# Attention, then routed experts: the weighted sum of a tile five steps behind its scores, with what goes along

## The chip, the cores and the metric

One core of a Trainium2 chip runs the whole program in one launch. Times are device microseconds of that core. The kernel before has a median of 1753.66 us over three runs (1752.63 to 1756.88).

## The reference

Four batches of 12288 queries (384 x 32 positions, 128 channels) attend to 768 keys each. The keys are the means of 4 x 4 blocks of `kv`, times a 128 x 128 matrix; the values are the same rows.

```
kv_flat = mean of 4x4 blocks of kv, @ w_sr          # [B, 768, 128]
k = v = kv_flat
s = (q @ k.T) / sqrt(128);  a = exp(s - max(s));  a /= sum(a) + 1e-9
x = a @ v                                            # [B * 12288, 128]
do = x @ w_skip > 0;  e = argmax(x @ w_gate);  g = softmax(x @ w_gate)[e]
out = x + do * g * (relu(x @ w1[e]) @ w2[e])         # 8 experts, 1024 hidden
```

The last two lines hold for rows of which `do` is true; the others are `x` itself. Of 49152 rows each goes to one of eight experts or to none.

## The kernel before, in words

A tile is 128 queries, so there are 384 tiles (`NTILE`), 96 in each batch (`TPB`). The work around the change is one loop over steps t (`while t < NTILE + LAG`), whose order on every engine is the order in which the loop writes its instructions. In step t:

- PE computes the scores of tile t (`scores`, six matmuls of 384 columns, since each factor is split in a high and a low half), then the weighted sum of tile t - `LAG` (`attend`, 18 matmuls of 138 columns: 128 value columns, nine projections for routing, one column of ones for the softmax's sum), then transposes the last two of the six key blocks of tile t-1 (`p_transpose`).
- DVE takes the row maximum of tile t (`row_max`), ACT its exponential (`row_exp`).
- Of tile t-1, ACT writes the high halves (f16) of the first four key blocks (`p_hi`), DVE the low halves (`p_lo`); then SP's queue gets a DMA that transposes both into `pt`. `attend` reads `pt` as weights. The pool `ptp` has `LAG` buffers of `pt`; the pool `hl` has four of `p16`, from which the DMA reads.
- The two blocks that PE transposed go to `ptq` for a pair of tiles at once: ACT copies the high halves and DVE subtracts, a step after the second tile of the pair was transposed (`next_a`, `next_v`).
- After each second `attend`, ACT scales the two tiles' sums to rows; after each fourth, SP stores them (`out_dram<-rows`); after each twelfth, a row job (`route`) starts, which ranks the rows of 12 tiles by expert over the following steps, on POOL, DVE and PE, and hands out the scatter of these rows to `scr` (`scatter_next`, one a step, on POOL's queue).
- Queries come in groups of four tiles: `load_q` at each fourth step on SP's queue, `q_split` into high and low halves some steps later.
- The next batch's `kv` comes as 24 loads of 256 KB on SP's queue (`KV_T`: six key blocks of four parts). POOL adds up the blocks (`pool_kv`, from four steps after the last part), and `prep_kv` makes keys and values of them from step 86 of the batch on, one piece a step (`preps`).

Ahead of the loop the first batch's keys are made; its values (`prep_v(0)`: largest key, scale, weight `wv`, two halves of value matmuls) are made in the first steps, one piece a step, and are needed by the first `attend`.

The last steps (t from 384) hold two attends a step and the first matmuls of the expert blocks: 24 peeled blocks of 512 rows of the largest expert (`peel`), then a loop over the rest. `first_step(left)` starts loading and splitting the experts' weights in the last 54 steps.

The lines that matter: `LAG` L66, `prep_v` L597, `p_transpose` L689, `attend` L708, the list of loads L966 and the step loop L977. Matmuls of `scores` are L655 to L657, of `attend` L720; `p_hi` is L673, `p_lo` L677, the transposing DMA L682, PE's transposes L695, the pair's copy and subtraction L702 and L703, the store L738, the value matmuls L591 with their copy L594 and subtraction L526, `wv` L549.

Of the kernel before, what the change touches and what calls it, by code (L numbers as in the profile page):

```python
# [14 lines left out]
AF = mybir.ActivationFunctionType  # L15
ALU = mybir.AluOpType
# [9 lines left out]
def kernel(  # L26
# [11 lines left out]
    nc = tc.nc  # L38
    NR, C, RT, P = q.shape
    B = kv.shape[0]  # L40
# [7 lines left out]
    PEXP = 15  # L48
# [10 lines left out]
    GT = 4  # L59
    GW = GT * P  # L60
    RG = RT // GT
    TPB = NQ // P
    NTILE = B * TPB
    NGRP = NTILE // GT
    XW = C + 10
    LAG = 6  # L66
    WARM = 6
    PREWARM = 7
    PSL = 11
    KD = 4  # L70
    PP = 2
# [352 lines left out]
    with ExitStack() as p1:  # L424
# [172 lines left out]
        def prep_v(b, c0=0):  # L597
            v_max(b, c0, KC)
            yield
            v_weight(b)  # L600
            yield
            yield
            for h in range(2):
                v_matmul(b, h)
                yield

        def prep_kv(b):
            for h in range(2):
                k_matmul(b, h * HC, (h + 1) * HC)
                yield  # L610
            yield from prep_v(b)
# [19 lines left out]
        def q_split(g):  # L631
            q_g = q_sb.pop(g)
            hi = qt.tile([P, GW], F32R, name="q_hi")
            lo = qt.tile([P, GW], F32R, name="q_lo")
            early_a.append(lambda: nc.scalar.copy(hi, q_g))

            def low():
                if g < 3:
                    behind(nc.gpsimd.tensor_tensor(out=lo, in0=q_g, in1=hi.bitcast(F32), op=ALU.subtract))
                    return  # L640
                paced["both"] = nc.vector.tensor_tensor(out=lo, in0=q_g, in1=hi.bitcast(F32), op=ALU.subtract).ins

            early_g.append(low)
            qT[g] = (hi, lo)
# [42 lines left out]
        KP = KC - KD  # L687

        def p_transpose(t):  # L689
            g, j = divmod(t, PP)  # L690
            if j == 0:
                PTP[g] = acc_ps()
            p = p_flat(t)
            for i in range(KP):
                nc.tensor.transpose(PTP[g][:, (j * KP + i) * P:(j * KP + i + 1) * P],  # L695
                                    p[:, (KD + i) * P:(KD + i + 1) * P], ident)
            if j < PP - 1:
                return
            ps = PTP[g][:, 0:PP * KP * P]
            hl_t = ptq.tile([P, 2, PP * KP * P], F16, name="ptq")  # L700
            PTQ[g] = hl_t.rearrange("p a (j k x) -> p a j k x", j=PP, x=P)
            next_a.append(lambda: nc.scalar.activation(out=hl_t[:, 0, :], in_=ps, func=AF.Copy, scale=2.0 ** PEXP))  # L702
            next_v.append(lambda: nc.vector.scalar_tensor_tensor(  # L703
                out=hl_t[:, 1, :], in0=ps, scalar=2.0 ** PEXP, in1=hl_t[:, 0, :], op0=ALU.mult, op1=ALU.subtract))

        AVL = [(k, v, x) for k in range(KC) for v, x in ((0, 0), (0, 1), (1, 0))]

        def attend(t):  # L708
            g, j = divmod(t, GT)
            r, o = divmod(g, RG)  # L710
            v_hi, v_lo, v_sc = *KV[t // TPB][2:4], KV[t // TPB][4][:, 0:1]
            v = (v_hi, v_lo)
            if j % 2 == 0:
                AVT[g] = acc_ps()[:, 0:2 * XW].rearrange("p (a x) -> p a x", x=XW)
            ps = AVT[g]
            pt = PT.pop(t)
            ptq_t = PTQ[t // PP]
            for i, (k, a, x) in enumerate(AVL):
                w = pt[:, x * KD + k, :] if k < KD else ptq_t[:, x, t % PP, k - KD, :]
                nc.tensor.matmul(ps[:, j % 2, :], w, v[a][:, k, :], start=(i == 0), stop=(i == len(AVL) - 1))  # L720
            if j == 0:
                if o == 0:
                    ROWS[r] = rowp.tile([P, RT, XW], F32, name="rows")
            rows = ROWS[r][:, o * GT:(o + 1) * GT, :]
            rs = small.tile([P, 2], F32, name="rs") if j % 2 == 1 else None

            def inverse():
                nc.vector.tensor_scalar(out=rs, in0=ps[:, :, XW - 1], scalar1=1e-9 * 2.0 ** PEXP, scalar2=v_sc,  # L728
                                        op0=ALU.add, op1=ALU.mult)
                nc.vector.reciprocal(rs, rs)  # L730

            def scale():
                for i in (0, 1):
                    c = j - 1 + i
                    nc.scalar.activation(out=rows[:, c, :], in_=ps[:, i, :], func=AF.Copy, scale=rs[:, i:i + 1])
                if j < GT - 1:
                    return
                nc.sync.dma_start(ov[r][:, o * GT:(o + 1) * GT, :], rows[:, :, 0:C])  # L738
                if o == RG - 1:
                    jobs.append([route(r), None])  # L740

            if j % 2 == 1:
                early_v.append(inverse)
                next_l.append(scale)
# [221 lines left out]
        KV_T = {}  # L966
        for nb in range(1, B):
            for i in range(KC * R):
                at = 7 * i // 4 if nb == 1 else (nb - 1) * TPB - 10 + 3 * i
                KV_T.setdefault(at, []).append((nb, *divmod(i, R)))  # L970
        PREP_T = 86
        PAD_T = [t for t in range(LAG, NTILE - 68) if t // TPB == B - 1 or t % TPB >= PREP_T]
        PAD_T = [PAD_T[i * len(PAD_T) // NPAD] for i in range(NPAD)]
        assert len(set(PAD_T)) == NPAD
        alloc["w"] = acc_ps
# [1 line left out]
        t = -1  # L977
        while t < NTILE + LAG:
            t += 1
            b, tb = divmod(t, TPB)  # L980
            live = t < NTILE
            for now, nxt in ((split_a, next_a), (split_v, next_v), (late_a, next_l)):
                now.extend(nxt)
                nxt.clear()
            if live:
                scores(t, range(t == 0, 2))
            for u in (t - LAG,) if live else (2 * t - NTILE - LAG, 2 * t - NTILE - LAG + 1):
                if 0 <= u < NTILE:
                    attend(u)
            if 0 <= t - 1 < NTILE:  # L990
                p_transpose(t - 1)
            if live:
                row_max(t)
            if t == 0:
                next(gate, None)
            run_late(early_a)
            run_late(split_a)
            if 0 <= t - 1 < NTILE:
                p_hi(t - 1)
            run_late(late_a)  # L1000
            if live:
                row_exp(t)
            run_late(split_v)
            run_late(early_v)
            if 0 <= t - 1 < NTILE:
                p_lo(t - 1)
            run_late(early_g)
            if live:
                if t % GT == 0 and t // GT + RG < NGRP:
                    load_q(t // GT + RG)  # L1010
                for nb, k, r in KV_T.get(t, ()):
                    load_kv(nb, k, [r])
                if b + 1 < B and tb == PREP_T:
                    preps.append(prep_kv(b + 1))
                if t in PAD_T:
                    write_pads(*PADS.pop(0))
            first_step(NTILE - t)
            if t == NTILE:
                p_s.close()
                p_kv.close()  # L1020
                first_p.append(p1.enter_context(tc.tile_pool(name="first_p", bufs=HOLD)))
                fill(p1, "fill5", 64)
                alloc_h(p1.enter_context(tc.tile_pool(name="hp1", bufs=1)))
                ps_up = p1.enter_context(tc.tile_pool(name="ps_up", bufs=4, space=PSUM))
                alloc["h"] = alloc["w"] = lambda: ps_up.tile([P, ST], F32, name="up_ps")
            ph = t % GT
            if ph == 1 and t // GT + 2 < NGRP:
                q_split(t // GT + 2)
            taken.clear()
            if live:  # L1030
                scatter_next()
            ranked = run_jobs(ph)
            if not live and (not taken or t >= NTILE + 4):
                scatter_next()
            if preps and not ranked and (ph != 0 or tb < LAG):
                if next(preps[0], "end") == "end":
                    preps.pop(0)
            if live and b + 1 < B:
                for nb, k, r in KV_T.get(t - 4, ()):
                    if r == R - 1:  # L1040
                        pools.append(pool_kv(nb, k))
                if pools and len(taken) < 2 and next(pools[0], "end") == "end":
                    pools.pop(0)
                assert not pools or tb < PREP_T, (t, len(pools))
            if 0 <= t - NTILE < FC // 2:
                next(first)
                next(first)
# [96 lines left out]
```

## Time and profile before

| | us |
|---|---|
| median of three runs | 1753.66 |
| the profiled execution | 1737.34 |
| its span, first to last instruction | 1735.6 |
| DVE busy | 1525.8 (88%) |
| ACT busy | 1265.2 (73%) |
| POOL busy | 1024.7 (59%) |

The span is read in three parts: up to about 23 us the first loads and keys, up to 951 us the steps of the attention loop, then the expert blocks. PE is TensorE's matmuls, PEld its weight loads, SP the queue from which most DMAs are issued. An engine's idle time is the time before an instruction in which it did nothing; the profile names beside it what ended the wait. TensorE's granted clock is 0.999 of full speed over the span.

### The profile page before, as it was taken

Reading aid. Unit: us, or ns where it says so; the run is one execution under the profiler, and the core shown is the slowest. Engines: PE = TensorE matmul, PEld = TensorE weight load, DVE = VectorE, ACT = ScalarE, POOL = GpSimd, SP = SyncE. Lnnn points to the kernel's source line nnn. Section 1 sums busy time; section 2 is a strip of 40 time slices with the busy share of each in tenths; the row PEclk is TensorE's granted clock in tenths of the full one; section 3 lists DMA queues with packets and bytes.
Section 4 is the critical chain, followed back from the end, with each engine's and each line's share of the span. In section 5 each row is a group of like instructions: output and inputs, shape, how many; then the busy total and the mean of one; then the engine's idle time right before and its main releaser. Section 6 shows DMA issues by size and latency. Waiting matters only on the chain.

```text
span 1735.6 us, 51351 instructions
## 1 busy us (share of the span) xinstructions
PE 1703.6 (98%) x18801; PEld 1426.6 (82%) x18801; DVE 1525.8 (88%) x3217; ACT 1265.2 (73%) x2399; POOL 1024.7 (59%) x1292
## 2 busy tenths in 40 slices
PE   6999999999999999999999999999999999999998
PEld 5999999999999989999999777777777777777776
DVE  7989999999999999999999877777888888888887
ACT  4888888888898888888888655555555556666664
POOL 3268878888788888765668445543333333343433
PEclk9999999999999999999999999999999999999999
DMA  8999999999899999999998666222433333333333
GB/s 239 220 242 204 198 199 228 228 200 184 175 194 206 226 218 202 183 199 198 203 202 186 175 193 149 89 83 75 93 102 103 99 97 99 100 107 101 97 99 86
DMA packets 616917, 281.18 MB, mean 162 GB/s; under 512 B 502944, under 2 KB 567072, under 8 KB 616736
## 3 DMA queue, kind: packets, MB, share of 16 engines
q1 hardware_dynamic: 590192, 231.68, 64.5%
q0 software_dynamic: 21504, 38.43, 7.0%
q10 hardware_dynamic: 5040, 8.72, 1.3%
q8 instruction: 106, 1.74, 0.5%
q14 instruction: 75, 0.61, 0.1%
HBM read 85.36 MB, written 79.72 MB: 95 GB/s over the span
## 4 chain that ended last, share of the span: by engine, by line
PE 82%; DVE 11%; DMA 2%; issue 2%; POOL 1%; ACT 1%; SPq 0%; POOLq 0%; DVEq 0%; ACTq 0%
PE acc_ps L311 22%; PE acc_ps L720 17%; PE s_ps L655 6%; PE s_ps L657 6%; PE s_ps L656 5%; PE h_ps L296 5%; PE h_ps L298 5%; PE h_ps L297 5%; DVE nm L663 4%; PE acc_ps L695 4%; PE up_ps L296 2%; PE up_ps L298 2%; PE up_ps L297 2%; DVE p L677 2%; DVE ptq L703 1%
## 5 line engine op out<-in xcount | busy, mean ns | idle before, releaser
L192 POOL DMA_INDIRECT scr<-rows,di x384 | 422.2, 1099 | 170.0 <-DVE nm L663 91.5
L669 ACT ACTIVATE p_sb<-s_ps,nm 128x768 f32<-128x768 f32 x384 | 346.8, 903 | 103.9 <-DVE nm L663 100.9
L192 POOL DMA_INDIRECT out_dram<-o,xin x196 | 201.6, 1029 | 318.5 <-DVE o L323 266.0
L663 DVE TENSOR_REDUCE nm<-s_ps 128x1 f32<-128x768 f32 x384 | 365.2, 951 | 19.0 <-PE s_ps L657 17.4
L299 ACT ACTIVATE h_hi<-h_ps 128x512 f16<-128x512 f32 x384 | 223.9, 598 | 206.9 <-PE h_ps L298 193.3
L720 PEld LDWEIGHTS <-pt 128*128 128x128 f16 x4608 | 274.8, 97 | 64.7 <-issue 63.0
L720 PE MATMUL acc_ps<-v_hi,pt 128*128 128x138 f16 x3072 | 320.1, 224 | 2.7 <-DVE rs L728 1.8
L311 PEld LDWEIGHTS <-h_hi 128*128 128x128 f16 x4608 | 287.6, 98 | 15.6
L655 PE MATMUL s_ps<-k_hi,q_hi 128*128 128x384 f32 x768 | 293.4, 382 | 0.4 <-ACT k_hi L520 0.4
L720 PE MATMUL acc_ps<-v_lo,pt 128*128 128x138 f16 x1536 | 293.0, 223 | 0.0
L677 DVE SCALAR_TENSOR_TENSOR p<-p_sb,p 128x512 f16<-128x512 f32 x384 | 276.9, 721 | 5.6 <-ACT p L673 4.8
L300 DVE SCALAR_TENSOR_TENSOR h_lo<-h_ps,h_hi 128x512 f16<-128x512 f32 x384 | 245.7, 687 | 19.4 <-ACT h_hi L299 17.9
L657 PE MATMUL s_ps<-k_hi,q_lo 128*128 128x384 f32 x768 | 259.4, 338 | 0.0
L656 PE MATMUL s_ps<-k_lo,q_hi 128*128 128x384 f32 x768 | 258.1, 336 | 1.0 <-DVE k_lo L521 1.0
L673 ACT ACTIVATE p<-p_sb 128x512 f16<-128x512 f32 x384 | 242.4, 631 | 12.5 <-DMA pt<-p 9.6
L311 PE MATMUL acc_ps<-w_hi,h_lo 128*128 128x128 f16 x2304 | 222.6, 219 | 0.0
L311 PE MATMUL acc_ps<-w_lo,h_hi 128*128 128x128 f16 x2304 | 210.9, 219 | 0.0
L311 PE MATMUL acc_ps<-w_hi,h_hi 128*128 128x128 f16 x2304 | 210.9, 219 | 0.0
L299 ACT ACTIVATE h_hi<-up_ps 128x512 f16<-128x512 f32 x192 | 114.5, 597 | 109.5 <-PE up_ps L298 100.9
L720 PE MATMUL acc_ps<-v_hi,ptq 128*128 128x138 f16 x1536 | 178.0, 223 | 0.0
L323 DVE SCALAR_TENSOR_TENSOR o<-acc_ps,g_sc,xin 128x128 f32<-128x128 f32 x288 | 81.0, 344 | 104.5 <-PE acc_ps L311 100.8
L720 PE MATMUL acc_ps<-v_lo,ptq 128*128 128x138 f16 x768 | 154.9, 223 | 0.0
(200 smaller groups left out, 3393.7 us busy)
## 6 DMA issues: line engine op xcount, KB each, us to landing
q_sb<-in_q_dram SPq DMA_DIRECT2D x96, 256.0 KB
out_dram<-rows SPq DMA_DIRECT2D x96, 256.0 KB
xin<-scr SPq DMA_DIRECT2D x75, 264.0 KB, 2.9
kvt<-in_kv_dram SPq DMA_DIRECT2D x74, 256.0 KB
w_raw<-in_moe_w_dram SPq DMA_DIRECT2D x26, 512.0 KB, 3.9
scr<-pad ACTq DMA_DIRECT2D x32, 264.0 KB
pt<-p SPq DMA_TRANSPOSE x384
scr<-rows,di POOLq DMA_INDIRECT x384
```

What stands on the lines that cost most here:

```text
L192: ins = nc.gpsimd.indirect_dma_start(out=dst, out_offset=bass.IndirectOffsetOnAxis(ap=ids, axis=0), in_=src, in_offset=None, bounds_check= ...
L299: nc.scalar.activation(out=h["hi"][:, c, :], in_=ps, func=AF.Relu)
L300: paced["by"] = nc.vector.scalar_tensor_tensor(out=h["lo"][:, c, :], in0=ps, scalar=0.0, in1=h["hi"][:, c, :], op0=ALU.max, op1=ALU.subtra ...
L311: m = nc.tensor.matmul(ys[t], h[x][:, k, t * P:(t + 1) * P], w[:, k, :], start=(i == 0), stop=(i == len(terms) - 1))
L655: nc.tensor.matmul(s[:, h, :HK], q_hi, k_hi[:, sl], start=True, stop=False)
L656: nc.tensor.matmul(s[:, h, :HK], q_hi, k_lo[:, sl], start=False, stop=False)
L657: nc.tensor.matmul(s[:, h, :HK], q_lo, k_hi[:, sl], start=False, stop=True)
L663: paced["by"] = nc.vector.tensor_reduce(out=NM[t], in_=S_PS[t][:, :, :HK], axis=AX.XY, op=ALU.max, negate=True).ins
L669: nc.scalar.activation(out=P_SB[t], in_=S_PS.pop(t)[:, :, :HK], func=AF.Exp, bias=NM.pop(t))
L673: nc.scalar.activation(out=P16[t][:, 0, :], in_=p_flat(t)[:, 0:KD * P], func=AF.Copy, scale=2.0 ** PEXP)
L677: paced["both"] = nc.vector.scalar_tensor_tensor(out=p16[:, 1, :], in0=p_flat(t)[:, 0:KD * P], scalar=2.0 ** PEXP, in1=p16[:, 0, :], op0=A ...
L720: nc.tensor.matmul(ps[:, j % 2, :], w, v[a][:, k, :], start=(i == 0), stop=(i == len(AVL) - 1))
```

## The change

- `LAG` is 5. So `attend(t - 5)` stands in step t, the pool of `pt` has five buffers, and the step loop is one step shorter.
- The phases that hang on the attends count from t + 1 instead of t: the split of queries (the first one stays at step 1), the row jobs, the pads, the start-up of the experts, and the steps in which pieces of `preps` may run. The start of a batch's `prep_kv` keeps its step (86); one piece is now allowed in a step that was skipped before.
- Pairs for `ptq` are tiles (1, 2), (3, 4), ... with tile 0 and tile 383 alone, instead of (0, 1), (2, 3), ...
- Loads of the second batch's `kv`: load i comes at step max(7i/4, 5i/2 - 6) instead of 7i/4. The first nine (i = 0 to 8) keep their steps, the last comes at step 51 instead of 40.
- In the first batch the two halves of the value matmuls come a step sooner (one empty piece less).

```diff
-    LAG = 6
+    LAG = 5
...
             v_weight(b)
             yield
-            yield
+            if b > 0:
+                yield
             for h in range(2):
                 v_matmul(b, h)
                 yield
...
         def p_transpose(t):
-            g, j = divmod(t, PP)
-            if j == 0:
+            g, j = divmod(t + 1, PP)
+            if g not in PTP:
                 PTP[g] = acc_ps()
...
-            if j < PP - 1:
+            if j < PP - 1 and t < NTILE - 1:
                 return
-            ps = PTP[g][:, 0:PP * KP * P]
+            sl = slice(0 if g else (PP - 1) * KP * P, (j + 1) * KP * P)
+            ps = PTP[g][:, sl]
...
-            ptq_t = PTQ[t // PP]
+            ptq_t = PTQ[(t + 1) // PP]
...
-                at = 7 * i // 4 if nb == 1 else (nb - 1) * TPB - 10 + 3 * i
+                at = max(7 * i // 4, 5 * i // 2 - 6) if nb == 1 else (nb - 1) * TPB - 10 + 3 * i
                 KV_T.setdefault(at, []).append((nb, *divmod(i, R)))
...
-        PAD_T = [t for t in range(LAG, NTILE - 68) if t // TPB == B - 1 or t % TPB >= PREP_T]
+        PAD_T = [t for t in range(LAG + 1, NTILE - 68) if t // TPB == B - 1 or t % TPB >= PREP_T]
...
-            b, tb = divmod(t, TPB)
             live = t < NTILE
+            t1 = t + 1
+            b, tb = divmod(t1, TPB)
...
-                if b + 1 < B and tb == PREP_T:
-                    preps.append(prep_kv(b + 1))
-                if t in PAD_T:
+                if t % TPB == PREP_T and t // TPB + 1 < B:
+                    preps.append(prep_kv(t // TPB + 1))
+                if t1 in PAD_T:
                     write_pads(*PADS.pop(0))
-            first_step(NTILE - t)
+            if not live:
+                first_step(NTILE - t)
+            elif t1 < NTILE:
+                first_step(NTILE - t1)
...
-            ph = t % GT
-            if ph == 1 and t // GT + 2 < NGRP:
-                q_split(t // GT + 2)
+            ph = t1 % GT
+            if t == 1 or (t > 1 and ph == 1 and t1 // GT + 2 < NGRP):
+                q_split(t1 // GT + 2)
...
-            if preps and not ranked and (ph != 0 or tb < LAG):
+            if preps and (tb == PREP_T + 2 or not ranked and (ph != 0 or t < LAG)):
                 if next(preps[0], "end") == "end":
                     preps.pop(0)
```

## Rows read from the trace of the kernel before

**Rows 1.** The page's first part: busy time, share of the span, instructions

```profile
PE 1703.6 (98%) x18801; PEld 1426.6 (82%) x18801; DVE 1525.8 (88%) x3217; ACT 1265.2 (73%) x2399; POOL 1024.7 (59%) x1292
```

**Rows 2.** Busy time by stretch: length, engines' busy us (instructions), clock, DMA share, GB/s

```profile
0.00:23.00 23.00, 10.33 (x33) 7.26 (x33) 13.19 (x18) 3.32 (x6) 10.99 (x43) 1.00 0.91 334
23.00:40.00 17.00, 14.51 (x112) 12.60 (x112) 15.51 (x28) 14.04 (x25) 5.50 (x6) 1.00 0.61 116
...
60.00:140.00 80.00, 78.90 (x863) 73.11 (x862) 73.31 (x142) 68.42 (x127) 46.25 (x71) 1.00 1.16 239
...
250.00:350.00 100.00, 100.00 (x1098) 93.30 (x1097) 95.45 (x185) 88.67 (x163) 81.33 (x110) 1.00 1.13 227
350.00:450.00 100.00, 99.72 (x1094) 92.80 (x1092) 96.96 (x187) 87.30 (x161) 84.15 (x108) 1.00 0.96 187
...
1600.00:1736.00 136.00, 127.22 (x1443) 92.72 (x1443) 108.34 (x250) 75.84 (x150) 53.37 (x52) 0.98 0.34 95
```

**Rows 3.** Timeline of PE: first matmuls of seven attends, and one transpose

```profile
52.98 0.29 PE L720 MATMUL acc_ps<-v_hi,pt 128*128 128x138 f16 x2
...
119.74 0.29 PE L720 MATMUL acc_ps<-v_hi,pt 128*128 128x138 f16 x2
...
120.83 0.38 PE L695 MATMUL acc_ps<-ident,p_sb 128*128 128x128 f32 x2
...
122.11 0.29 PE L720 MATMUL acc_ps<-v_hi,pt 128*128 128x138 f16 x2
...
125.16 0.29 PE L720 MATMUL acc_ps<-v_hi,pt 128*128 128x138 f16 x2 [0.31 <-DMA pt<-p]
...
308.72 0.29 PE L720 MATMUL acc_ps<-v_hi,pt 128*128 128x138 f16 x2
...
615.67 0.29 PE L720 MATMUL acc_ps<-v_hi,pt 128*128 128x138 f16 x2
...
852.55 0.29 PE L720 MATMUL acc_ps<-v_hi,pt 128*128 128x138 f16 x2
```

**Rows 4.** List of waits, the span: us in total, times, longest us

```profile
ACT p L673 <- DMA pt<-p: 9.6, 16, 1.6
...
PE acc_ps L807 <- POOL oh_all L766: 1.8, 1, 1.8
...
PE acc_ps L720 <- DMA pt<-p: 0.7, 2, 0.4
```

**Rows 5.** Timeline of ACT: five `p_hi` and the idle time before each

```profile
54.37 0.63 ACT L673 ACTIVATE p<-p_sb 128x512 f16<-128x512 f32 x1 [0.92 <-DMA pt<-p]
...
125.19 0.63 ACT L673 ACTIVATE p<-p_sb 128x512 f16<-128x512 f32 x1 [1.40 <-DMA pt<-p]
...
309.86 0.63 ACT L673 ACTIVATE p<-p_sb 128x512 f16<-128x512 f32 x1 [0.65 <-DMA pt<-p]
...
616.14 0.63 ACT L673 ACTIVATE p<-p_sb 128x512 f16<-128x512 f32 x1 [0.22 <-DMA pt<-p]
853.12 0.63 ACT L673 ACTIVATE p<-p_sb 128x512 f16<-128x512 f32 x1 [0.34 <-DMA pt<-p]
```

**Rows 6.** Timeline of the first steps, all engines

```profile
28.55 0.41 ACT L549 ACTIVATE wv<-w_dn,v_x_sc 128x138 f32<-128x138 f32 x1 [0.79 <-DVE v_x_sc L547]
...
30.68 0.58 ACT L702 ACTIVATE ptq<-acc_ps 128x512 f16<-128x512 f32 x1
...
30.83 0.44 PE L695 MATMUL acc_ps<-ident,p_sb 128*128 128x128 f32 x2 [1.53 <-ACT p_sb L669]
...
31.11 0.87 PE L591 MATMUL acc_ps<-wv,pooled 128*128 128x138 f32 x6
...
32.47 0.51 ACT L594 COPY kvf<-acc_ps 128x414 f32<-128x414 f32 x1
...
36.04 0.91 POOL L526 TENSOR_TENSOR v_lo<-kvf,v_hi 128x411 f16<-128x411 f32 x1
```

**Rows 7.** Timeline of PE where attention hands over to the experts

```profile
960.45 0.29 PE L720 MATMUL acc_ps<-v_hi,pt 128*128 128x138 f16 x2 [0.41 <-DMA pt<-p]
```

More of the change, by code (lines that the diff above doesn't have):

```diff
@@ L696, in p_transpose @@
                                     p[:, (KD + i) * P:(KD + i + 1) * P], ident)
-            if j < PP - 1:
+            if j < PP - 1 and t < NTILE - 1:
                 return
-            ps = PTP[g][:, 0:PP * KP * P]
+            sl = slice(0 if g else (PP - 1) * KP * P, (j + 1) * KP * P)
+            ps = PTP[g][:, sl]
             hl_t = ptq.tile([P, 2, PP * KP * P], F16, name="ptq")
             PTQ[g] = hl_t.rearrange("p a (j k x) -> p a j k x", j=PP, x=P)
-            next_a.append(lambda: nc.scalar.activation(out=hl_t[:, 0, :], in_=ps, func=AF.Copy, scale=2.0 ** PEXP))
+            next_a.append(lambda: nc.scalar.activation(out=hl_t[:, 0, sl], in_=ps, func=AF.Copy, scale=2.0 ** PEXP))
             next_v.append(lambda: nc.vector.scalar_tensor_tensor(
-                out=hl_t[:, 1, :], in0=ps, scalar=2.0 ** PEXP, in1=hl_t[:, 0, :], op0=ALU.mult, op1=ALU.subtract))
+                out=hl_t[:, 1, sl], in0=ps, scalar=2.0 ** PEXP, in1=hl_t[:, 0, sl], op0=ALU.mult, op1=ALU.subtract))
         AVL = [(k, v, x) for k in range(KC) for v, x in ((0, 0), (0, 1), (1, 0))]
@@ L716, in attend @@
             pt = PT.pop(t)
-            ptq_t = PTQ[t // PP]
+            ptq_t = PTQ[(t + 1) // PP]
             for i, (k, a, x) in enumerate(AVL):
-                w = pt[:, x * KD + k, :] if k < KD else ptq_t[:, x, t % PP, k - KD, :]
+                w = pt[:, x * KD + k, :] if k < KD else ptq_t[:, x, (t + 1) % PP, k - KD, :]
                 nc.tensor.matmul(ps[:, j % 2, :], w, v[a][:, k, :], start=(i == 0), stop=(i == len(AVL) - 1))
@@ L1043 @@
                     pools.pop(0)
-                assert not pools or tb < PREP_T, (t, len(pools))
+                assert not pools or t % TPB < PREP_T, (t, len(pools))
             if 0 <= t - NTILE < FC // 2:
```

## The prediction

> **What bounds the kernel now.** I began with the page's first part. TensorE (PE) works 98% of the span [rows 1], so a change can only win time by removing the 32 us in which PE does nothing, and it loses time wherever it makes PE wait. The table of busy time by stage says where those 32 us are [rows 2]: 12.7 us before 23 us, 2.5 us between 23 and 40 us, 8.4 us after 1600 us (the span ends at 1735.6 us), and so only 8.4 us in all the rest. The first stage is loading, and the last is the end of the expert loop; the change touches neither. What it can reach is the head from 23 to 40 us, the steps of the attention loop (one tile each, 2.37 us, which is the distance of two attends in [rows 3], 119.74 to 122.11), and the few steps in which that loop hands over to the expert blocks at 951 us.
>
> Then I read the list of waits. The one that bears on the change is not PE's. ACT waits 16 times, 9.6 us in all, 1.6 us at most, for the DMA that transposes the probabilities (`pt<-p`) [rows 4]. `p_hi` of tile u+4 writes over the buffer from which tile u's transpose reads (`hl` has four), so ACT's wait dates the landing of tile u's transpose in the step u+5. Today PE wants that transpose in step u+6, a step later, and hardly ever waits. With LAG 5 it wants it in step u+5, when ACT does.
>
> **The parts of the change.** *Five tiles behind instead of six.* PE issues no instruction less. The place of `attend(u)` is that of `attend(u-1)` today. So the lateness of each transpose is the time of ACT's release [rows 5] minus the start of the attend before it [rows 3]:
> - tile 8: 54.37 - 52.98 = 1.4 us
> - tile 37, the worst: 125.16 (when PE itself waited 0.31 us for it) - 122.11 = 3.1 us
> - tile 113: 309.86 - 308.72 = 1.1 us
> - tile 240: 616.14 - 615.67 = 0.5 us
> - tile 337: 853.12 - 852.55 = 0.6 us
>
> These are the peaks of five bursts; the other eleven waits lie inside the same bursts or are smaller. When PE has been delayed by a burst's peak, everything behind it is delayed alike, so that within one burst the peak counts and not the sum. PE has no slack to make it up. With all five paid the price is 6.7 us.
>
> *Later keys' loads spread.* This edit works against the one before. Loads of the second batch's keys came at steps 0 to 40 and now come at steps 0 to 51; behind the first nine, one every 2.5 steps instead of every 1.75. The first nine keep their steps, so tile 8's burst keeps its cause. Tile 37's burst comes at the end of the dense loads. The share of the DMA engines is 1.16 in 60:140, 1.13 in 250:350, where a load comes every three steps, and 0.96 in 350:450, where the loads run out [rows 2]. The new rate is near that of 250:350, whose worst lateness was the 1.1 us of tile 113. So the first batch pays between 1.4 us (the early burst alone) and 4.5 us (both bursts in full); I take 1.5 us, close to the early burst, since the remaining loads are close to the regime whose peak is smaller than that. The other batches keep their loads: 1.1 + 0.5 + 0.6 = 2.2 us. Together 3.7 us. From this goes what PE loses to the same cause today, 1.1 us in 60:140 [rows 2]. Net +2.6 us, between -1.1 us (no transpose late any more) and 6.7 - 1.1 = +5.6 us with one payment a burst.
>
> *Phases.* The split of q, the pairs of PE transposes, the row jobs, the pads and the start-up of the experts move a step forward together with the attends; the pairs change parity because the attends do. So the buffers in PSUM and the loads of ACT and DVE in even and odd steps keep their distance. One thing doesn't: the store of four finished tiles now comes one step behind the q load on SP's queue, ahead of that step's transpose, where it was two behind. Both stand in front of the transpose of one tile in four. I put no term on it; it is a reason for the upper bound and the slower rival below.
>
> *The head.* Tile 0's pair is now a single, so its copy by ACT and subtraction by DVE move from step 3 (30.68, 0.58 us for the pair [rows 6]) to step 2, at half the width: between 0.29 and 0.58 us, I take 0.4. The first values' matmuls come a step sooner: 0.87 us of PE (31.11) ahead of the scores of tile 3, not tile 4. They need `wv`, which ACT ends at 28.96; the scores of tile 3, queued behind them on PE, would begin at 29.8. PE idles 1.53 us until 30.83 there today, so that delay costs little. But ACT's copy of the values (0.51 us at 32.47) also moves forward, ahead of tile 3's exponential, while the 0.58 us of the pair leave that step. ACT's chain is so later by 0.4 + 0.51 - 0.58 = 0.3 us. PE has one attend more behind it at step 7 than today, 1.09 us (119.74 to 120.83 in [rows 3]), and these few steps are paced by exponentials, not by PE. What idle time is left in which that attend fits I put at 0.4 us; less the 0.3 us it gives -0.1 us. The bounds are -1.1 us (it fits whole) and +0.9 us (the two ACT items delay all that follows). The values themselves are there in time: the last `v_lo` is ready at 36.95 today and would be some 2 us earlier, with the attend at step 5, a step earlier too.
>
> *The hand-over.* After the last scores PE has one attend less to do, 1.09 us, and the end would come sooner by that if nothing else were waited for. But at 960.45 PE has already waited 0.41 us for the transpose of tile 381 [rows 7], and what must happen before it (exponential, split, transpose) follows from the last scores. So the saved attend there mostly turns into waiting: +0.5 us beside the shift counted above, between 0 and +1.1 us. The three steps' jobs that now run at a different place of the expert blocks run beside the 24 peeled expert blocks, all of them ahead of the loop that needs their result, and cost nothing; without that cover they would show as SP waiting ahead of the first block of the loop.
>
> **The sum.** +2.6 - 0.1 + 0.5 = +3.0 us on the profiled execution of 1737.34 us (span 1735.6 us): 1740.3 us. The timed runs have a median of 1753.66 us, 16.3 us or 0.9% above the profiled one; the profile doesn't say where that lies, so I add the same difference: 1756.7 us. What a measurement can tell from no change is 0.3%, 5.3 us; +3.0 us lies inside.
>
> **The rivals.** *The cover holds.* If the spread loads bring every transpose in time, PE loses nothing to them, also not today's 1.1 us, and the attend at the head fits whole: -1.1 - 1.1 = -2.2 us, 1751.5 us. For it: of 384 transposes ACT waited for 16, and the worst came at the end of the dense loads, which are thinned. Against it: tiles 113, 240 and 337 were late under loads that the change doesn't touch. The Trainium skill, page "DMA: Bandwidth & Descriptors", section "Anatomy of one DMA — SWDGE (gpsimd) path", has a rule that would favour this rival: a fixed 2.0 us plus the bytes at 436 GB/s, stated for the GpSimd path. For the 256 KB of one tile it gives an estimate of 2.6 us from issue to landing, little more than a step, in every tile alike; issued at the end of step u+1 and wanted in step u+5, none would be late, and the time would be this rival's, 1751.5 us. The waits on `pt<-p` show some landing three steps later than that, so the trace doesn't agree.
>
> *Every burst charges each of its waits.* On the slower side: PE now stops in the same step as ACT, SP's next transposes are issued later for that, and the next tile is late again instead of being carried by the delay. Then PE pays the 9.6 us of ACT's 16 waits one by one [rows 4], less today's 1.1 us, and the hand-over: 8.5 - 0.1 + 0.5 = +8.9 us, 1762.6 us. For it: the store that now follows the q load closely, and a DMA share above 1.1 through a third of the loop [rows 2]. Against it: while PE waits, the queue drains. It decides from about 6 us of waiting on `pt<-p` by PE upward (5.3 + 1.1 us, less the head and the hand-over), since less is within 0.3%.
>
> *More is saved than the head.* PE's largest single stop in the loop is 1.8 us, for the one-hot rows from GpSimd [rows 4]; it may vanish when the row jobs move, or come back elsewhere (bounds -1.8 and +1.8 us, taken as nothing). For a gain above 5.3 us most of the 8.4 us in the middle would have to go, and nothing in the change aims at them: 1748 us at best.
>
> **How the numbers follow.** The forecast has 0.50, the cover that holds 0.25, the waits charged one by one 0.17, the large gain 0.08. A part of the first reaches over 5.3 us when the second and third peaks are paid in full, and a part of the slower rival stays under it. So: faster 0.09, same 0.69, slower 0.22. Of the range, the lower end is the cover that holds with GpSimd's stop gone as well, 1749.7 us; the upper end is the slower rival and the upper bounds of head and hand-over, +8.9 + 1.0 + 0.6 = 1764.2 us. I say 1749.5 to 1764.5.
>
> **What would show it.** The list of PE's waits should have PE waiting for `pt<-p` some 3 to 5 us in all (0.7 us today [rows 4]), in few pieces, the first near 53 us and one near 310 us, and ACT's 16 waits should go, since PE's stop covers them. Between 60 and 140 us the idle time of PE should not be much above 1.5 us. In the head, attends begin near 34.7 us and scores of tile 7 near 38.6 us. I am wrong if PE waits for `pt<-p` less than 1 us (the cover holds), if it waits over 6 us, or if the time changes at another place, such as GpSimd's one-hot rows or the first block of the expert loop.

## The result, and the profile after

The changed kernel takes 1765.94 us (median of 6 runs, 1763.94 to 1766.99); the kernel before, run beside it on the same chip, takes 1754.25 us (6 runs, 1752.63 to 1756.88). The ratio is 1.0065, with a 95% interval of 1.0052 to 1.0078: slower, by 11.7 us. The prediction said 1756.7 us, 3.0 us over before and no change that can be measured, with a range that ended at 1764.5 us. It was wrong, on the side of the slower rival, whose 1762.6 us is nearer to what was measured.

The profiled execution of after took 1764.59 us (span 1762.9 us). Part 1 of its page (busy time, share, instructions), against [rows 1]:

```profile
PE 1710.9 (97%) x18801; PEld 1428.3 (81%) x18801; DVE 1520.5 (86%) x3218; ACT 1265.8 (72%) x2400; POOL 1017.6 (58%) x1292
```

The table of busy time by stage (stretch, its length, busy time and instructions of PE, PEld, DVE, ACT, POOL, then the granted clock as a share, the DMA share and GB/s), of after, against [rows 2]:

```profile
23.00:40.00 17.00, 14.12 (x106) 12.17 (x107) 14.74 (x29) 13.46 (x24) 6.32 (x6) 1.00 0.60 104
60.00:140.00 80.00, 79.96 (x882) 74.35 (x879) 75.25 (x146) 69.61 (x129) 49.36 (x73) 1.00 1.13 228
140.00:250.00 110.00, 107.32 (x1160) 99.05 (x1159) 99.85 (x200) 92.49 (x172) 83.30 (x115) 1.00 1.03 200
250.00:350.00 100.00, 98.16 (x1067) 91.16 (x1065) 93.55 (x182) 86.40 (x159) 79.25 (x107) 1.00 1.09 216
350.00:450.00 100.00, 99.44 (x1096) 92.53 (x1095) 95.81 (x183) 87.37 (x161) 83.61 (x108) 1.00 0.97 190
450.00:600.00 150.00, 148.10 (x1597) 136.69 (x1596) 139.65 (x275) 128.59 (x237) 116.50 (x158) 1.00 0.97 197
```

In 60 to 140 us PE now idles 0.04 us, less than the 1.1 us of [rows 2]. From there on it idles where it hardly did: 2.7, 1.8, 0.6 and 1.9 us in the next four stretches. The list of waits of after (us in total, times, longest) says for what, against [rows 4]:

```profile
PEld L722 <- DMA pt<-p: 15.8, 23, 3.5
...
PE acc_ps L311 <- issue: 10.5, 15, 1.2
...
PE acc_ps L722 <- DMA pt<-p: 8.4, 10, 3.3
```

PE waits for the transposed probabilities in two places of its pipeline: where it loads them as weights (PEld, 15.8 us) and, when the matmuls before have run out too, in the matmuls (8.4 us). The first figure is the better clock of lateness, the second is nearer to what PE loses. The second line of the fence, 10.5 us in the expert blocks, looked like a part of the loss; the first experiment is about it.

Which transposes were late? I numbered the attends by their weight loads (384 of them) and sorted the 23 waits by the tile: 20 are of tiles whose number is divisible by four, with 15.0 of the 15.8 us. So SP's instructions around such a tile are the place to look. SP's queue of after (start, time, operation, count):

```profile
151.12 1.23 SPq L683 DMA_TRANSPOSE pt<-p  x1
152.40 0.57 SPq L622 DMA_DIRECT2D q_sb<-in_q_dram  x1
153.07 0.39 SPq L740 DMA_DIRECT2D out_dram<-rows  x1
153.56 8.49 SPq L683 DMA_TRANSPOSE pt<-p  x4
```

and the same place in the queue of before:

```profile
141.88 1.37 SPq L621 DMA_DIRECT2D q_sb<-in_q_dram  x1
143.78 1.24 SPq L682 DMA_TRANSPOSE pt<-p  x1
145.11 0.53 SPq L738 DMA_DIRECT2D out_dram<-rows  x1
145.75 5.88 SPq L682 DMA_TRANSPOSE pt<-p  x3
```

In before, a transpose goes out between the load of q and the store of four finished tiles, and the one behind the store is that of tile 49: there the store stands ahead of the tiles that leave a remainder of one when divided by four. In after the two stand one behind the other, and the transpose behind both, the first of the four from 153.56 us on, is that of tile 52. PE's weight loads of after, of tiles 51 and 52 and then of tiles 100, 104 and 116 (in brackets the idle time ahead and its releaser):

```profile
157.70 0.71 PEld L722 LDWEIGHTS <-pt 128*128 128x128 f16 x12 [0.16 <-issue]
160.81 0.71 PEld L722 LDWEIGHTS <-pt 128*128 128x128 f16 x12 [0.90 <-DMA pt<-p]
...
281.38 0.71 PEld L722 LDWEIGHTS <-pt 128*128 128x128 f16 x12 [0.60 <-DMA pt<-p]
291.89 0.71 PEld L722 LDWEIGHTS <-pt 128*128 128x128 f16 x12 [1.04 <-DMA pt<-p]
321.46 0.71 PEld L722 LDWEIGHTS <-pt 128*128 128x128 f16 x12 [1.15 <-DMA pt<-p]
```

A gap of 0.16 us stands there at a tile that waits for nothing, too; eight of the 23 waits are hardly longer than that (0.16 to 0.24 us), and the other fifteen carry the sum. Tile 52's transpose let PE go on at 160.81 us, 7.25 us after SP began to issue it. The DMA packets in the same trace show what stood ahead of it: on SP's queue tile 51's transpose ends at 156.29 us, the q load (128 packets of 2 KB) runs to 157.17 us, the store (512 packets of 512 B) to 157.92 us, and only then come tile 52's packets of 256 B, to about 159.0 us. The two transfers take 1.6 us there, more than the 0.90 us for which PE waits. The Trainium skill, page "DMA: Bandwidth & Descriptors", section "Queues, rings and completion order", states that each DMA engine takes the descriptors of a ring in order. The trace agrees: these packets run in the order in which SP issued them. SP also began the issue 1.2 us after the low halves of tile 52 were ready (152.36 us), since it was issuing the other two until then; no run separates the two delays.

Standing behind a store isn't enough to be late: 94 transposes do, and 13 of them made PE's weight loads wait for more than 0.25 us. The packets give a part of the reason. Between 40 and 975 us there are 58 stops of 1.1 to 2.8 us, in which several packets of SP's queue took over 1 us each, where the median of a transpose's packets is 18 ns. Such a stop falls between issue and use for 46 of the 94, and for 10 of the 13. What causes these stops was not tried.

### The profile page after: what moved, and what is told of

It reads as the page before. It is cut to its first block, busy times and chain, and to the rows that moved or that the text cites. A ratio compares the mean times of both kernels' runs of the same rounds, so it can differ in the third digit from the quotient of the medians.

```text
span 1762.9 us, 51399 instructions
## 1 busy us (share of the span) xinstructions
PE 1710.9 (97%) x18801; PEld 1428.3 (81%) x18801; DVE 1520.5 (86%) x3218; ACT 1265.8 (72%) x2400; POOL 1017.6 (58%) x1292
## 4 chain that ended last, share of the span: by engine, by line
PE 88%; DVE 4%; DMA 4%; issue 2%; POOL 1%; ACT 0%; SPq 0%; POOLq 0%; DVEq 0%
PE acc_ps L311 22%; PE acc_ps L722 21%; PE s_ps L656 7%; PE s_ps L658 6%; PE s_ps L657 6%; PE h_ps L296 5%; PE h_ps L298 5%; PE h_ps L297 5%; PE acc_ps L696 4%; DMA pt<-p 3%; PE up_ps L296 2%; PE up_ps L297 2%; PE up_ps L298 2%; DVE nm L664 1%; DVE p L678 1%
## 5 line engine op out<-in xcount | busy, mean ns | idle before, releaser
L678 DVE SCALAR_TENSOR_TENSOR p<-p_sb,p 128x512 f16<-128x512 f32 x384 | 271.7, 707 | 2.8 <-ACT p L674 1.5
L300 DVE SCALAR_TENSOR_TENSOR h_lo<-h_ps,h_hi 128x512 f16<-128x512 f32 x384 | 245.8, 688 | 19.3 <-ACT h_hi L299 16.3
L311 PEld LDWEIGHTS <-h_lo 128*128 128x128 f16 x2304 | 152.9, 98 | 8.8 <-issue 8.8
```

The costliest lines, as they stand in the source:

```text
L300: paced["by"] = nc.vector.scalar_tensor_tensor(out=h["lo"][:, c, :], in0=ps, scalar=0.0, in1=h["hi"][:, c, :], op0=ALU.max, op1=ALU.subtra ...
L311: m = nc.tensor.matmul(ys[t], h[x][:, k, t * P:(t + 1) * P], w[:, k, :], start=(i == 0), stop=(i == len(terms) - 1))
L678: paced["both"] = nc.vector.scalar_tensor_tensor(out=p16[:, 1, :], in0=p_flat(t)[:, 0:KD * P], scalar=2.0 ** PEXP, in1=p16[:, 0, :], op0=A ...
```

## The experiments

Ratios are to the kernel before, run on the same chip; they are taken over the runs, not from the medians, from whose quotient they differ by up to 0.08%. The first eight ran on two chips on which it takes 1754.06 us (23 runs) and 1753.75 us (35 runs).

**Before, once more.** No edit. Is the wait of 10.5 us in the expert blocks the change's, or the chip's?

> The kernel before, profiled once more. The changed kernel's profile has 10.5 us of PE waiting for nothing visible (issue) in the down matmuls L311 of the peeled expert blocks; the first profile of before has none, but its execution (1737.3 us) also lies 16 us below the median of its own timed runs. Theory A: these waits are not the change's, and most executions of before have them too: this profile shows 8 to 14 us of issue waits at L311 and a time near 1753 us. Rival B: the change causes them: this profile shows none again, and a time near 1737 us.

It took 1756.42 us (span 1754.4 us). Its list of waits:

```profile
PE acc_ps L311 <- issue: 10.5, 12, 1.2
...
ACT p L673 <- DMA pt<-p: 10.2, 12, 2.9
```

The same 10.5 us are there without the change, so they are no part of its loss. They are missing in the first trace of before, and that was a profile 16.3 us under the median. This execution is therefore the one to set beside after's, though it lies 2.4 us over the median of its kernel and after's 1.4 us under its own, so that the parts below come out rather too small. The stretches by PE's marks (the first score of tile 7, the last scores of tile 383, the end) give:

- to tile 7's scores 39.48 instead of 37.71 us, +1.8 us; since one attend (1.09 us) more has been done by then, +0.7 us
- from there to the last scores 923.8 instead of 919.9 us, +3.9 us
- from there to the end 799.5 instead of 796.7 us, +2.8 us; with one attend less to do there, +3.9 us

Together +8.5 us, the difference of the two spans; the other 3.2 us of the 11.7 lie between these executions and the medians of their runs. By PE's idle time the middle term is +5.8 us in 140 to 600 us (6.98 against 1.15 us), -2.2 us in 60 to 140 us (0.04 against 2.27 us) and +0.5 us behind.

**The q load moved, the store moved, and the loads of before.** Three edits of after, each taking back one suspect. The q load a step off the store:

```
-if t % GT == 0 and t // GT + RG < NGRP:
-    load_q(t // GT + RG)
+if (t == 0 or t1 % GT == 0) and t1 // GT + RG < NGRP:
+    load_q(t1 // GT + RG)
```

> The changed kernel with the q load issued a step earlier too, so that on SP's queue it is again two steps ahead of the store instead of directly ahead of it. Theory collision: four steps are too short only for the one tile in four (u = 0 mod 4) whose transpose stands right behind the q load and the store; weight loads' waits for pt fall from 15.8 us to under 6 us and the time by 5 to 9 us, to about 1758 us. Rival distance: four steps are too short for transposes at large, whatever stands ahead; waits stay above 12 us and the time within 3 us of 1766 us.

The store issued behind the step's transpose instead of ahead of it:

```
-nc.sync.dma_start(ov[r][...], rows[:, :, 0:C])
+stores.append(lambda: nc.sync.dma_start(ov[r][...], rows[:, :, 0:C]))
...
+run_late(stores)
```

> The changed kernel with the store of four tiles issued behind the step's transpose instead of ahead of it. Theory collision: the transpose of the tile 0 mod 4 then has only the q load ahead, the store falls on the next tile; waits for pt fall from 15.8 us to under 8 us, the long wait of 3.3 us at the hand-over (tile 380, behind a store) goes to under 1 us, time about 1757 to 1760 us. Rival distance: the wait moves on to the tiles 1 mod 4, waits stay above 12 us, time within 3 us of 1766 us.

The second batch's keys loaded as before:

```
-at = max(7 * i // 4, 5 * i // 2 - 6) if nb == 1 else (nb - 1) * TPB - 10 + 3 * i
+at = 7 * i // 4 if nb == 1 else (nb - 1) * TPB - 10 + 3 * i
```

> The changed kernel with the second batch's loads at their old steps (7i/4). Theory of the prediction: the spread relieves the transposes between 60 and 140 us; without it PE's idle time there rises from 0.04 us to 2 to 4 us and the time by 2 to 3 us, to 1768 to 1769 us. Rival: the spread does nothing for the time (the total of DMA work is the same and the late transposes are those behind the store): within 1 us of the changed kernel.

Measured: q load moved, 1759.47 us, ratio 1.0028 [1.0018, 1.0037]; store moved, 1756.23 us, 1.0011 [1.0001, 1.0020]; loads of before, 1768.24 us, 1.0076 [1.0061, 1.0092]. The first two times are near what the collision was expected to give. From the lists of waits, the q load moved:

```profile
PEld L722 <- DMA pt<-p: 8.2, 9, 3.6
```

the store moved:

```profile
PEld L722 <- DMA pt<-p: 6.4, 7, 2.6
```

Moving the store by one place in one queue, with no instruction more or less, brings back 9.5 of the 11.7 us; moving the other neighbour brings back 6.3 us. The waits of the q-load kernel stay above the expected 6 us, since 3.6 of the 8.2 us are one wait at the hand-over. Of the store-moved kernel's 7 waits 5 are still of tiles divisible by four, and the longest (2.6 us, expected under 1 us) is at the hand-over. SP's queue of that kernel shows a transpose between the two again:

```profile
151.96 0.57 SPq L622 DMA_DIRECT2D q_sb<-in_q_dram  x1
152.63 2.46 SPq L683 DMA_TRANSPOSE pt<-p  x1
155.18 0.53 SPq L740 DMA_DIRECT2D out_dram<-rows  x1
```

With the loads of before, the median is 2.3 us above after's, but the intervals overlap; its first dense stretch shows more than the median does:

```profile
60.00:140.00 80.00, 76.57 (x814) 70.71 (x812) 70.18 (x136) 65.69 (x122) 44.07 (x67) 0.98 1.10 225
```

PE idles 3.4 us there, against 0.04 us in after. The spread loads do work against the late transposes, in their own stretch: the two kernels of the next group that have them idle there for at most 0.1 us.

**Alone, and together.** The spread in the kernel before; q load and store both moved in after; and, in the kernel before, the neighbourhood alone (q load at `t % GT == 1`, directly ahead of the store, still six tiles):

> The kernel before with one part of the change alone: the second batch's loads at max(7i/4, 5i/2 - 6). If the spread relieves the transposes, PE's idle time in 60:140 (1.1 and 2.3 us in two profiles of before) falls under 0.5 us and ACT's waits for pt in 50:140 mostly go; the time falls by 1 to 2.5 us against before, 0.1%. Rival: the relief is used up by the longer stretch of loads: time within 0.5 us of before, waits appear between 130 and 165 us.

> The changed kernel with both repairs, the q load a step earlier and the store behind the step's transpose. If the neighbours ahead of one transpose were the cause, q load and store are now two transposes apart and PE's and its weight loads' waits for pt in the loop fall below 3 us (12.3 us in the changed kernel, 4.6 and 3.9 us with one repair); the hand-over still waits about 2.4 us, since xT's transpose stands ahead of tile 380's; time 1753 to 1756 us, no slower than with the store alone. Rival: what is left after one repair is the missing step, which no order brings back: the same 1756 us and 4 us of waits.

> The kernel before with LAG 6 and the q load one step later, so that q load and store stand directly ahead of one transpose as they do in the changed kernel. If it takes both the neighbours and the missing step, the late transposes are hidden here: PE's waits for pt stay below 4 us, ACT's rise above 15 us, and the time is within 2 us of before. Rival: the neighbours alone cost the time: 5 us or more slower than before.

Measured: 1753.66 us, 0.9992 [0.9983, 1.0000]; 1755.82 us, 1.0009 [1.0000, 1.0018]; 1755.47 us, 1.0009 [1.0000, 1.0018]. The lists of waits, both moved:

```profile
PEld L722 <- DMA pt<-p: 2.5, 3, 1.9
```

the neighbourhood alone, at six tiles:

```profile
ACT p L673 <- DMA pt<-p: 3.8, 8, 1.0
...
PEld L720 <- DMA pt<-p: 1.2, 1, 1.2
```

SP's queue of the last one shows that the neighbours stand as in after:

```profile
145.20 0.57 SPq L621 DMA_DIRECT2D q_sb<-in_q_dram  x1
145.86 0.40 SPq L738 DMA_DIRECT2D out_dram<-rows  x1
146.36 7.64 SPq L682 DMA_TRANSPOSE pt<-p  x4
```

So it takes both. Five tiles without the neighbourhood cost 0.09%, the neighbourhood with six tiles costs 0.09%, each at the limit of its interval; the two together, with the hand-over, cost 0.65%. With six tiles PE's weight loads wait for no transpose in the loop (the one wait is at the hand-over): the step that the sixth tile gave was what hid the queue. One expectation failed: ACT's waits were to rise above 15 us and are 3.8 us, fewer than the 9.6 and 10.2 us of before, though six of the eight are of tiles directly behind the two. How late the transposes are there is therefore not shown by ACT. The spread alone removes PE's idle time in 60 to 140 us (0.00 us), but the time did not fall by the expected 1 to 2.5 us: the medians differ by 0.1 us. And in the neighbourhood kernel, which loads the keys as before, PE's idle time there is 0.00 us too, so at six tiles the spread isn't the only edit that relieves this stretch.

**The hand-over.** In after the longest wait of all is where the loop ends. SP's queue of after:

```profile
962.19 1.30 SPq L289 DMA_TRANSPOSE xT<-x  x1
963.59 0.53 SPq L740 DMA_DIRECT2D out_dram<-rows  x1
964.22 6.70 SPq L683 DMA_TRANSPOSE pt<-p  x4
```

Tile 380's transpose stands behind the store and behind the transpose of the experts' first inputs (`xT`), which moved a step forward with the steps' jobs. In before the same two stand ahead of tile 381's, which PE wants later and for which it waits 0.41 us [rows 7]:

```profile
953.09 1.26 SPq L289 DMA_TRANSPOSE xT<-x  x1
954.44 0.54 SPq L738 DMA_DIRECT2D out_dram<-rows  x1
955.08 4.95 SPq L682 DMA_TRANSPOSE pt<-p  x3
```
PE of after:

```profile
970.33 0.36 PE L722 MATMUL acc_ps<-v_hi,pt 128*128 128x138 f16 x2 [3.33 <-DMA pt<-p]
```

The next kernels issue the `xT` transposes earlier, one with q load and store moved as well, one with this edit alone, and one with the old lag, the spread loads and this edit:

```
-W1_AT, X0_AT = (19, 13, 11, 9), (9, 7, 5, 3)
+W1_AT, X0_AT = (19, 13, 11, 9), (12, 10, 8, 6)
```

> As the kernel with both repairs, and the first expert block's x is split and transposed three steps earlier, so that its DMA (xT) no longer stands just ahead of tile 380's transpose. If that transpose makes the wait at the hand-over, it falls from about 2.4 us to under 0.7 us, the granted clock between 951 and 1000 us stays at 1.00 instead of 0.97, and the time falls by 2 to 4 us, to 1750 to 1753 us, below the kernel before. Rival: the wait follows from the chain of the last tiles itself (exponential, split, transpose): it stays above 1.5 us and the time where it was.

> The changed kernel with only the first expert block's x split and transposed three steps earlier. At the hand-over tile 380's transpose still stands behind a store, no longer behind xT's DMA: PE's wait there falls from 3.3 us to between 1 and 2 us; the loop's 12.3 us of weight-load waits stay; time 2 to 3 us below the changed kernel, 1763 us. Rival: the neighbours of the loop also make the wait at the hand-over: it stays near 3 us and the time near 1765.5 us.

> The kernel before (LAG 6) with the two parts that helped: the spread loads and the earlier x of the first expert block. If the shorter distance is worth nothing on its own, this is as fast as or faster than the version with LAG 5 and all repairs (1752.5 us): 1751 to 1753 us. If LAG 5 is worth its one attend of PE time (1.1 us) once its transposes are in time, this one is slower by that, 1753.5 us.

With all three moved: 1752.53 us, 0.9990 [0.9981, 0.9999], 3.3 us less than with two. PE hardly waits for a transpose any more:

```profile
PEld L722 <- DMA pt<-p: 1.4, 2, 0.9
```

`xT` alone and the old lag ran on another chip, on which before takes 1737.1 us (18 runs): 1744.36 us, 1.0035 [1.0023, 1.0048], and 1737.42 us, 1.0000 [0.9991, 1.0008]. In the first the wait at the hand-over is 1.73 us instead of 3.33 us, and the ratio is 0.3% below after's, but after itself was not run on that chip. 18 of its 19 PEld waits are still of tiles divisible by four:

```profile
PEld L722 <- DMA pt<-p: 10.3, 19, 2.1
```

So the hand-over is a cause of its own, beside the one in the loop.

**Five against six, both repaired, on one chip.** The versions of the last two groups (all three edits at five tiles; spread and `xT` at six), unchanged and side by side:

> The version with LAG 5 and all three repairs once more, now beside the one with LAG 6 on the same chip. If the earlier 0.9990 [0.9981, 0.9999] is real it is again 0.998 to 1.000 of before; if it was the luck of one chip, 1.000 to 1.002.

> The version with LAG 6, spread loads and the earlier x, on the same chip as the repaired LAG 5. If LAG 5 is worth one attend of PE time once repaired, this one is 1 us slower than it; if the head and the hand-over take that back, the two lie within 0.5 us of each other.

Before takes 1754.59 us there; five tiles 1753.41 us, 0.9993 [0.9984, 1.0002]; six tiles 1752.51 us, 0.9988 [0.9978, 0.9999]. Waits for a transpose by PE: one of 0.9 us at five tiles, none at six, where ACT bears them:

```profile
ACT p L673 <- DMA pt<-p: 4.0, 7, 1.1
```

The smaller distance is worth nothing that these runs can tell. Nor is it shown that the two other edits win anything: the six-tile version, 0.12% faster than before here, is the same kernel that gave 1.0000 on the other chip, and the five-tile one gave 0.9990 and 0.9993 on two.

## Why the prediction was wrong, point by point

**The step that failed is the one on phases:** "the store of four finished tiles now comes one step behind the q load on SP's queue, ahead of that step's transpose, where it was two behind. ... I put no term on it". The place was seen and no price was put on it. It decided the result: undoing it brings back 9.5 us (store) or 6.3 us (q load), and the two together 9.6 us (from 11.7 to 2.1 us above before). Between the profile of after and those of these kernels the loop is shorter by 4.3 us (store) and 7.6 us (both), and what follows it by 1.8 and 3.2 us. PE's waits for the transposes came to 8.4 us, over the 6 us that the prediction had named as a sign of being wrong.

**The lateness was read in the old order of SP's queue.** The sum priced tiles 8, 37, 113, 240 and 337 by the lateness that they had there. ACT's waits were put down to the load on the DMA engines; the queue's order was in them too, since nine of the 16 were of tiles directly behind the store, 37, 113 and 337 among them. With the order changed nearly all late tiles are divisible by four. In the first batch little comes of it: nothing near 53 us, and at most 0.36 us at once before 140 us, where 1.4 us and then up to 3.1 us were feared. With the loads of before tile 36 waits 2.9 us, so the spread is what hides that one; near 53 us nothing is late with either. The three later places have their stops, by PE's weight loads: tile 116 with 1.15 us (113 was priced 1.1 us), tile 240 with 1.21 us (0.5 us), tile 336 with 0.90 us (0.6 us). What the sum lacks are nine more stops of 0.4 to 1.5 us between 160 and 930 us, 7.0 us together, eight of them of tiles divisible by four. The loop's net term, +2.6 us, came out +3.9 us between the two executions: the early part better than priced (-2.2 us against the execution of before, by the spread), the rest worse (+5.8 us in 140 to 600 us, where 2.2 us stood for all three later peaks).

**"Within one burst the peak counts and not the sum"** failed with it: tile 104 is late again, and by more, four tiles after PE has stopped for tile 100. Each stop is paid anew. That is nearer to the rival in which every wait is charged, in its sign and its total (1762.6 us); but that rival's tiles, ACT's sixteen, were not the ones (of them only tile 240 makes PE wait for more than 0.25 us), and ACT's waits didn't go: 4.2 us in 7 remain in after.

**The spread** was right: it works against the late transposes in 60 to 140 us (0.04 us of idle time with it, 3.4 us without it) and costs nothing alone (0.9992).

**The head** was -0.1 us, between -1.1 and +0.9 us, and came out +0.7 us: inside. Attends begin at 34.65 us, as foreseen (34.7), but the first stops for the values' low half, which the working had ready some 2 us sooner than before's 36.95 us. GpSimd and PE of after:

```profile
35.09 1.40 POOL L526 TENSOR_TENSOR v_lo<-kvf,v_hi 128x411 f16<-128x411 f32 x1
...
36.54 0.22 PE L722 MATMUL acc_ps<-v_lo,pt 128*128 128x138 f16 x1 [1.06 <-POOL v_lo L526]
```

It took 1.40 us instead of 0.91 us [rows 6] and ended at 36.49, 0.5 us sooner, and so the scores of tile 7 begin at 39.48 instead of near 38.6 us.

**The hand-over** was +0.5 us, at most +1.1 us, and came out +3.9 us. The mechanism was right in its kind (the saved attend turns into waiting for a transpose) and the size wrong: the wait of 3.33 us is three times the 1.09 us saved, since the working took the chain from the last scores to the transpose and left out what SP's queue holds there: `xT` and the store stand ahead of tile 380. The sentence that jobs at another place of the expert blocks "cost nothing" failed here for SP's part of them. Issuing `xT` earlier brought back 3.3 us on top of the two other edits. That the end is as much as 3.9 us late has a second part, the granted clock, told below.

**The 16.3 us** between the profile of before and the median were added unread, and rightly: the chip of that profile isn't on record, but its time and its missing stops in the expert blocks are those of the one fast chip. **GpSimd's rows** were neutral as taken: PE's stop of 1.8 us for them [rows 4] is 0.8 us in after.

What stays open: the loop of before differed by 6.1 us between two executions (913.8 and 919.9 us), more than the loop's own loss of 3.9 us, and the other six-tile kernels on the slower chips have loops of 914.1 to 918.5 us. The part of each stretch is therefore only as good as these two profiles; the parts of each edit rest on the timed runs.

## What to carry to other kernels

When a consumer is moved nearer to its producer, read the queue that carries the data in the new order, instruction by instruction, and price the transfer that stands directly behind others; the lateness that today's waits show belongs to the old order. A spare step is a cover for every neighbour in that queue: here either the neighbours or the missing step cost 0.09%, about what can be told from nothing, and the two with the hand-over 0.65%. And before the profile of before is set beside that of after, take a second one on the chip of the comparison.

## What the runs showed of the hardware

**One kernel, two times.** Before takes 1737.1 us on one chip and about 1754 us on three others. Between the two executions of before 12.5 us of the difference lie in the expert blocks that are written out, from the second of the 24 on (245.0 against 257.5 us). On the slower chips PE stops there, for nothing that the profile shows, in ten blocks in a row, between 1043 and 1161 us in the second execution of before: these take 11.6 to 12.6 us each, the others mostly 10.5 us. The timeline of the second execution of before, PE:

```profile
1063.53 0.33 PE L311 MATMUL acc_ps<-w_hi,h_hi 128*128 128x128 f16 x3 [1.25 <-issue]
...
1075.41 0.33 PE L311 MATMUL acc_ps<-w_hi,h_lo 128*128 128x128 f16 x3 [0.96 <-issue]
...
1087.16 0.27 PE L311 MATMUL acc_ps<-w_hi,h_lo 128*128 128x128 f16 x2 [0.99 <-issue]
```

and the stretch of 1000 to 1260 us in it, where the first execution of before has PE busy for 258.90 us:

```profile
1000.00:1260.00 260.00, 248.24 (x2792) 179.64 (x2789) 185.28 (x448) 139.14 (x281) 115.92 (x117) 1.00 0.40 112
```

What PE waits for there was not tried.

**A stall that cost twice.** After the stop of 3.33 us at the hand-over, the granted clock of after, in the table by stage:

```profile
965.00:970.00 5.00, 2.00 (x32) 1.80 (x29) 4.50 (x11) 3.84 (x7) 1.64 (x2) 1.00 1.32 145
970.00:975.00 5.00, 4.67 (x33) 3.53 (x34) 0.96 (x3) 0.82 (x2) 1.82 (x4) 0.66 0.57 134
```

It is 0.66 for the 5 us behind the stop, so a part of them ran at 1.2 GHz instead of 2.4 GHz; by an estimate from this row that is a third of 5 us, 1.7 us. At the same place a stop of 2.38 us (store moved) was followed by 0.68 in 965 to 970 us, one of 1.73 us (`xT` alone) by 1.00. With all three edits, where PE stops for 0.44 us there, 951 to 1000 us has PE busy for 48.56 of 49 us at a granted clock of 1.00, where after has 44.44 us at 0.97.
